# A chunked recurrence rewritten around 64x64 quadrants of TensorE, in units of eight pairs

## The chip, the cores and the metric

One core of one Trainium2 chip. The metric is the device time of one execution in microseconds; the kernel before is run three times and its median counts. Engines are named as in the profile: PE (TensorE), PEld (its weight loads), DVE (VectorE), ACT (ScalarE), POOL (GpSimd), SP (SyncE, which issues the DMAs).

## The reference

Three stages follow each other. The first is a recurrence over 768 tokens for 32 independent heads (4 batches x 8 heads), each with a 40x40 state; the other two are dense blocks over its output.

```python
for t in range(768):                       # state: [4, 8, 40, 40]
    y[t]  = r[t] @ state
    Sa    = state @ a[t]
    state = state * w[t] - outer(Sa, b[t]) + outer(v[t], k[t])
x = y rearranged to [4, 768, 320]
x = x + (gelu(x @ w_in)[u] * (w_sg @ layernorm(...)[v] + b_sg)) @ w_out   # [768 x 768] mixing over tokens
h = relu(x @ w_in2);  out = (h * sigmoid(conv3(h))) @ w_out2
```

## The kernel before

The function attention() does the recurrence, moe() the two dense blocks. The change is in attention() and in the host layout that feeds it; moe() is not touched.

The 768 tokens are cut into 12 chunks of 64. Within a chunk the recurrence becomes matrix products: decays are multiplied up along the chunk, the products of a and the decayed b and k give strictly triangular 64x64 matrices, a triangular system per head is solved, and the state is carried to the next chunk. Two heads form a pair (P = 0 and 1, on partitions 0 to 63 and 64 to 127), so there are 16 pairs; each chunk (hg) is two halves (q) of eight pairs, 24 halves in all. Two chunks form a group g (six groups), and one triangular solve serves a whole group.

- prep(hg): loads w twice (forward and reversed, tile w), a (at) and b, k (kbt); DVE runs two scans for each half (L94, L97) and multiplies at by the decay (L100); POOL multiplies kbt by the other decay (L102); ACT squares both for a range guard (L107). The tiles at are a ring of two, kbt is a ring of one.
- products(hg): PE multiplies kbt by at as 128x128 matmuls whose off-diagonal operand blocks are zero (gk, L124), DVE masks them into la (L127), PE transposes kbt (pkb, L130), ACT copies that to kbn.
- solve_a(g): DVE transposes la in 32x32 blocks (mu, L161), eliminates in 30 steps of two instructions (L168, L170), and transposes twice (tn L174, tt L176). It is a generator; each yield is a place at which the written-out order may continue with other work.
- solve_b(g, tq): PE and ACT complete the 64x64 inverse (pn L189, n L195, pt L201, tt L206), and ACT copies at into la (L207), after which the ring slot of at may be loaded anew.
- chain(g, c4): py, ys, pz, vz, pS, st (L224 to L249): the carried state of one half of a chunk; then pzt (L252). spart transposes the state (p, L262). ypart makes the output: gh (L276), ghs (L280), pyo (L285, L287), xo (L290), and stores it to x in DRAM (L295).

A list ORDER says in which order these parts are issued for one group; a scheduler then orders the instructions of each engine when the program is built, with higher priority for chain. All loads and stores go through SP's one queue.

```python
ORDER = ["chain 0", "chain 1", "g1", "sp 0", "a", "a", "a", "a", "y 0", "a", "a", "a", "sp 1", "a", "a", "y 1",
         "py0", "a", "a", "a", "chain 2", "chain 3", "a", "a", "a", "b0", "p0", "sp 2", "y 2", "g0", "sp 3", "y 3",
         "py1", "b1", "p1"]
```

Of the kernel before, what the change touches and what calls it, by code (L numbers as in the profile page):

```python
# [22 lines left out]
def attention(ctx, tc, ident, gu, wp, wr, a, kb, r, vt, v, x):  # L23
# [6 lines left out]
    D, C, J = 40, 64, 4  # L30
    NH = wp.shape[0]
# [3 lines left out]
    ps_g = ctx.enter_context(tc.tile_pool(name="ps_g", bufs=3, space=PSUM))  # L35
    ps_a = ctx.enter_context(tc.tile_pool(name="ps_a", bufs=2, space=PSUM))
    ps_c = ctx.enter_context(tc.tile_pool(name="ps_c", bufs=3, space=PSUM))
# [3 lines left out]
    p4 = ctx.enter_context(tc.tile_pool(name="a_p4", bufs=4))  # L41

    def ring(name, n, shape, val, engine, part=None):

        ts = [const.tile(shape, F32, name=f"{name}{i}") for i in range(n)]
        for t in ts:
            engine.memset(t if part is None else t[:, part:], val)
        return lambda i: ts[i % n]

    first = ring("first_", 1, [128, 8, 65], 0.0, nc.gpsimd)(0)  # L50
    rat = ring("at_", 2, [128, 16, 2, C], 0.0, nc.vector)
    rkbt = ring("kbt_", 1, [128, 16, 2, C], 0.0, nc.gpsimd)
    mask = const.tile([128, C], F32, name="mask")
    nc.gpsimd.memset(mask, 1.0)
    half = [slice(0, 64), slice(64, 128)]
    for h in half:
        nc.gpsimd.affine_select(out=mask[h], in_=mask[h], pattern=[[1, C]], compare_op=ALU.is_gt,
                                fill=0.0, base=0, channel_multiplier=-1)
    rtt = ring("tt_", 2, [128, 8, J, C], 0.0, nc.gpsimd)
    las = [const.tile([128, 2, 8, J, C], F32, name=f"la_{i}") for i in range(2)]  # L60
    rys = ring("ys_", 2, [128, 8, 2, C], 0.0, nc.gpsimd)
    rst = ring("st_", 2, [128, 8 * D + 24], 0.0, nc.gpsimd, 8 * D)
    rs0 = ring("s0_", 3, [128, 8 * D + 24], 0.0, nc.gpsimd, 8 * D)
    rr2 = ring("r2_", 3, [128, 8, 2, C], 0.0, nc.gpsimd)
    real = [slice(64 * P, 64 * P + D) for P in range(2)]
    given = [slice(64 * P, 64 * P + 48) for P in range(2)]
    rq = lambda q: slice(32 * q, 32 * q + 32)
    heads = [(i, P) for i in range(8) for P in range(2)]
    m8 = mask[:, None, None, :].to_broadcast([128, J, 2, C])

    tl, grp = {}, {}
# [4 lines left out]
    def prep(hg):  # L76

        at, kbt = rat(hg), rkbt(hg)
        px = p4.tile([128, 16, 65], F32, name="px")
        ws = []  # L80
        for src, nm in ((wp, "w1"), (wr, "w2")):
            for q in range(2):
                t = p2.tile([128, 8, 65], F32, name=nm)
                for P in range(2):
                    nc.sync.dma_start(out=flat(t)[half[P]], in_=src[hg, P, :, 520 * q:520 * q + 520])
                ws.append(t)
        for P in range(2):
            nc.sync.dma_start(out=at[given[P], :, P], in_=a[hg, P].rearrange("e (n t) -> e n t", t=C))
            nc.sync.dma_start(out=kbt[given[P]].rearrange("p n c t -> p (n c t)"), in_=kb[hg, P])
        for q in range(2):  # L90
            ns = slice(8 * q, 8 * q + 8)
            w1, w2 = ws[q], ws[2 + q]
            nc.vector.memset(first[:, :, 0], 1.0)
            nc.vector.tensor_tensor_scan(out=flat(px[:, ns]), data0=flat(w1), data1=flat(first), initial=0.0,  # L94
                                         op0=ALU.mult, op1=ALU.add)
            nc.vector.reciprocal(first[:, :, 0], px[:, ns, 64])
            nc.vector.tensor_tensor_scan(out=flat(w2), data0=flat(w2), data1=flat(first), initial=0.0,  # L97
                                         op0=ALU.mult, op1=ALU.add)
            for P in range(2):
                nc.vector.scalar_tensor_tensor(out=at[half[P], ns, P], in0=at[half[P], ns, P], scalar=-1.0,  # L100
                                               in1=px[half[P], ns, 0:C], op0=ALU.mult, op1=ALU.mult)
            nc.gpsimd.tensor_tensor(out=kbt[:, ns], in0=kbt[:, ns],  # L102
                                    in1=w2[:, :, C - 1::-1][:, :, None, :].to_broadcast([128, 8, 2, C]), op=ALU.mult)
            for i, t in enumerate((flat(px[:, ns]), flat(w2))):
                junk = p1.tile([128, 8 * 65], F16, name="junk")
                u = 4 * hg + 2 * q + i
                nc.scalar.activation(out=junk, in_=t, func=AF.Square, scale=2.0 ** -32, accum_out=gu[:, u:u + 1])  # L107
        tl[hg] = dict(px=px, at=at, kbt=kbt)

    def products(hg):  # L110

        g, tq = divmod(hg, 2)
        if tq == 0:
            grp[g] = dict(la=las[g % 2])
        la = grp[g]["la"]
        d = tl[hg]
        at, kbt = d["at"], d["kbt"]
        kbn = p4.tile([128, 16, 2, C], F32, name="kbn")
        for c in range(4):
            ns = slice(4 * c, 4 * c + 4)  # L120
            pg = ps_g.tile([128, J, 2, C], F32, name="gk", tag="pg")
            for j in range(J):
                n = 4 * c + j
# [3 lines left out]
            nc.vector.tensor_tensor(out=la[:, :, 4 * tq + c].rearrange("p P j t -> p j P t"), in0=pg, in1=m8, op=ALU.mult)  # L127
            pa = ps_a.tile([128, 4, 128], F32, name="pkb", tag="pa")
            for j in range(J):
                nc.tensor.transpose(out=pa[:, j], in_=kbt[:, 4 * c + j].rearrange("p c t -> p (c t)"), identity=ident)  # L130
            nc.scalar.activation(out=kbn[:, ns].rearrange("p n P e -> p n (P e)"), in_=pa, func=AF.Copy)  # L131
        cs = slice(4 * tq, 4 * tq + 4)
        for P in range(2):
            rows = rq(2 * P + 1)
            nc.gpsimd.tensor_copy(la[rows, P, cs, :, 0:32], la[rows, P, cs, :, 32:64])  # L135
        d.update(kbn=kbn)

    def prep_v(hg):
        vz = p2.tile([128, 2, 2, 8, D], F32, name="vz")
        for P in range(2):  # L140
            nc.sync.dma_start(out=vz[half[1 - P], P].rearrange("p q n e -> p (q n e)"), in_=v[hg, P])
        tl[hg].update(vz=vz)

    rv = {}

    def prep_y(n):
        hg, q = divmod(n, 2)
        cs = slice(512 * q, 512 * q + 512)
        r2 = rr2(n)
        zv = p3.tile([128, 8, 2, C], F32, name="zv")  # L150
        for P in range(2):
            nc.sync.dma_start(out=r2[given[P], :, P], in_=r[hg, P, :, cs].rearrange("e (n t) -> e n t", t=C))
            nc.sync.dma_start(out=zv[half[P], :, 1 - P], in_=vt[hg, P, :, cs].rearrange("e (n t) -> e n t", t=C))
        rv[n] = r2, zv

    def solve_a(g):

        la, tt = grp[g]["la"], rtt(g)
        mu = p1.tile([128, 32, 32], F32, name="mu")
        for P in range(2):  # L160
            nc.vector.transpose(out=mu[half[P]], in_=la[half[P], P, :, :, 0:32].rearrange("p c j t -> p t c j"))  # L161
        tmp = p1.tile([128, 240], F32, name="mtmp")
        for j in range(1, 31):
            if j % 3 == 0:
                yield
# [7 lines left out]
        tn = p1.tile([128, 8, J, 32], F32, name="tn")  # L173
        nc.vector.transpose(out=tn.rearrange("p c j i -> p i c j"), in_=mu.rearrange("p t i -> p i t"))  # L174
        yield
        nc.vector.transpose(out=tt[:, :, :, 32:64].rearrange("p c j t -> p t c j"), in_=mu)  # L176
        for P in range(2):
            nc.gpsimd.tensor_copy(tt[rq(2 * P), :, :, 0:32], tt[rq(2 * P), :, :, 32:64])
        grp[g].update(tt=tt, tn=tn)

    def solve_b(g, tq):

        la, tt, tn = (grp[g][n] for n in ("la", "tt", "tn"))
        cs = slice(4 * tq, 4 * tq + 4)
        pn = ps_a.tile([128, 4, J, 32], F32, name="pn", tag="pa")
        for c in range(4):
            for j in range(J):
                for P in range(2):
# [23 lines left out]
    def state(t):  # L212
        return t[:, 0:8 * D].rearrange("p (n e) -> p n e", e=D)

    def chain(g, c4):
        tq, q = divmod(c4, 2)
        hg = 2 * g + tq
        la, tt = grp[g]["la"], grp[g]["tt"]
# [92 lines left out]
    for n in range(3):  # L311
        prep_y(n)
# [491 lines left out]
```

## Time and profile before

| | |
|---|---|
| three runs | 1179.95, 1182.58, 1183.28 us; median 1182.58 |
| the profiled execution | 1181.11 us; its span 1179.4 us |
| mean granted PE clock | 0.85 of 2.4 GHz |
| busy share of the span | PE 73%, PEld 67%, DVE 63%, ACT 36%, POOL 20% |
| moved by DMA | 69.33 MB, 83,696 of 103,650 packets under 512 B |

The span is the time from the first to the last instruction of the profile; the execution's own time adds what lies around it (1.7 us here). The recurrence fills the first 682 us of the span, the dense blocks the remaining 497 us. A matmul of float32 operands appears as two records of PE and two of PEld.

### The profile page before, as it was taken

To read this page: it belongs to the slowest core of one execution; us is meant where nothing else is said; L and a number is where in the kernel's file an instruction comes from. 1 tells how busy PE (TensorE), PEld (TensorE's weight loads), DVE (VectorE), ACT (ScalarE), POOL (GpSimd) and SP (SyncE) were. 2 spreads that over 40 slices of the span, in tenths; PEclk is the share of its full clock that TensorE was granted. 3 is DMA by queue.
4 is the path that set the end of the run, shared out by engine and by line. 5 is a ranking of instruction groups with operands and counts; after the bars stand their busy time and mean duration, and the time that the engine had idled before them with its cause. 6 is when DMAs were issued, how large, how long until landed. Compare 5 with 4: busy or idle time off the path is not lost.

```text
span 1179.4 us, 23401 instructions
## 1 busy us (share of the span) xinstructions
PE 856.1 (73%) x9777; PEld 793.6 (67%) x9777; DVE 748.6 (63%) x1348; ACT 428.5 (36%) x839; POOL 236.9 (20%) x223
## 2 busy tenths in 40 slices
PE   2306670967488286929759937999999879989995
PEld 2305660856377275827758826999999879889984
DVE  6574259359746935874592267875555887776664
ACT  2302320332241133223313334432222337767764
POOL 5211101020202102020200034311111433223322
PEclk9656795879697787959788968999999989999998
DMA  9621241154233516232221195100000320000001
GB/s 160 125 54 37 48 93 34 33 105 93 61 69 61 108 28 110 62 79 59 38 64 27 29 254 150 41 1 1 1 1 1 101 78 1 34 18 18 18 17 37
DMA packets 103650, 69.33 MB, mean 59 GB/s; under 512 B 83696, under 2 KB 91376, under 8 KB 102384
## 3 DMA queue, kind: packets, MB, share of 16 engines
q1 hardware_dynamic: 103536, 67.75, 26.2%
q8 instruction: 79, 1.29, 0.5%
q14 instruction: 35, 0.29, 0.1%
HBM read 59.86 MB, written 7.86 MB: 57 GB/s over the span
## 4 chain that ended last, share of the span: by engine, by line
PE 43%; DVE 24%; DMA 13%; ACT 7%; issue 7%; POOL 3%; SPq 2%; DVEq 0%; POOLq 0%; ACTq 0%
PE pv L595 6%; PE gk L124 4%; DMA at<-in_c_a 4%; PE ph L546 3%; PE pu L577 3%; DVE mtmp L168 3%; DVE mu L170 3%; PE pr L616 3%; PE p L680 3%; PE pzt L252 3%; PE gh L276 3%; DMA w<-in_c_wp 2%; PE pz L231 2%; DVE cv L686 2%; DMA raw<-in_moe_w_in 2%
## 5 line engine op out<-in xcount | busy, mean ns | idle before, releaser
L189 PE MATMUL pn<-tn,la 32*32 32x32 f32 x768 | 18.9, 214 | 157.0 <-DVE tn L174 155.7
L189 PEld LDWEIGHTS pn<-tn,la 32*32 32x32 f32 x768 | 17.5, 129 | 159.3 <-issue 156.9
L124 PE MATMUL gk<-at,kbt 128*128 128x128 f32 x384 | 68.9, 330 | 45.7 <-POOL kbt L102 32.3
L124 PEld LDWEIGHTS gk<-at,kbt 128*128 128x128 f32 x384 | 60.4, 237 | 49.2 <-POOL kbt L102 32.7
L102 POOL TENSOR_TENSOR kbt<-kbt,w 128x1024 f32<-128x1024 f32 x24 | 56.2, 2359 | 168.6 <-DMA w<-in_c_wp 109.4
L100 DVE SCALAR_TENSOR_TENSOR at<-at,px 64x512 f32<-64x512 f32 x48 | 44.0, 952 | 66.1 <-DMA at<-in_c_a 59.0
L689 POOL TENSOR_TENSOR cv<-cv,hz 128x384 f32<-128x384 f32 x64 | 57.7, 909 | 134.6 <-ACT cv L688 134.6
L168 DVE TENSOR_TENSOR mtmp<-mu 128x30 f32<-128x30 f32 (+9 forms) x180 | 67.0, 372 | 5.0
L170 DVE TENSOR_TENSOR mu<-mu,mtmp 128x30 f32<-128x30 f32 (+9 forms) x180 | 64.8, 360 | 5.0
L207 ACT ACTIVATE la<-at 64x1024 f32<-64x1024 f32 x24 | 25.2, 1052 | 110.1 <-PE pn L189 63.1
L595 PE MATMUL pv<-sg_hi,vh 128*128 128x384 f32 x192 | 64.5, 336 | 1.0 <-ACT vh L569 1.0
L595 PE MATMUL pv<-sg_lo,vh 128*128 128x384 f32 x192 | 64.5, 336 | 0.0
L595 PE MATMUL pv<-sg_hi,vl 128*128 128x384 f32 x192 | 63.8, 336 | 0.0
L599 POOL TENSOR_TENSOR g<-g,u 128x384 f32<-128x384 f32 x32 | 36.7, 1148 | 133.2 <-DVE g L598 128.7
L135 POOL COPY la<-la 32x512 f32<-32x512 f32 x24 | 14.6, 608 | 240.7 <-DVE la L127 218.2
L693 DVE TENSOR_TENSOR gl<-cv,gh 128x384 fp32r<-128x384 f32 x64 | 40.4, 636 | 33.1 <-ACT gh L692 33.0
L280 DVE TENSOR_TENSOR ghs<-gh,mask 128x512 f32<-128x512 f32 x48 | 32.7, 682 | 44.4 <-PE gh L276 26.7
L285 PE MATMUL pyo<-r,s 128*64 128x64 f32 x704 | 56.8, 247 | 3.1 <-ACT n L195 1.9
L127 DVE TENSOR_TENSOR la<-gk,mask 128x512 f32<-128x512 f32 x48 | 33.0, 687 | 41.1 <-PE gk L124 40.9
L131 ACT ACTIVATE kbn<-pkb 128x512 f32<-128x512 f32 x48 | 28.6, 595 | 81.1 <-PE pkb L130 80.6
L287 PE MATMUL pyo<-ghs,kbn 128*64 128x64 f32 x768 | 57.0, 240 | 0.0
L684 DVE SCALAR_TENSOR_TENSOR cv<-hz,cw,cv 128x384 f32<-128x384 f32 x64 | 40.7, 644 | 25.5 <-ACT cv L683 25.4
(151 smaller groups left out, 2471.6 us busy)
## 6 DMA issues: line engine op xcount, KB each, us to landing
kbt<-in_c_kb SPq DMA_DIRECT2D x24, 384.0 KB
w<-in_c_wp SPq DMA_DIRECT2D x48, 130.0 KB
w<-in_c_wr SPq DMA_DIRECT2D x48, 130.0 KB
zv<-in_c_vt SPq DMA_DIRECT2D x48, 128.0 KB
at<-in_c_a SPq DMA_DIRECT2D x24, 192.0 KB
r<-in_c_r SPq DMA_DIRECT2D x48, 96.0 KB
raw<-in_moe_w_in SPq DMA_DIRECT2D x8, 512.0 KB
vz<-in_c_v SPq DMA_DIRECT2D x24, 160.0 KB
```

The costliest lines, as they stand in the source:

```text
L100: nc.vector.scalar_tensor_tensor(out=at[half[P], ns, P], in0=at[half[P], ns, P], scalar=-1.0, in1=px[half[P], ns, 0:C], op0=ALU.mult, op1= ...
L102: nc.gpsimd.tensor_tensor(out=kbt[:, ns], in0=kbt[:, ns], in1=w2[:, :, C - 1::-1][:, :, None, :].to_broadcast([128, 8, 2, C]), op=ALU.mult)
L124: nc.tensor.matmul(out=pg[:, j].rearrange("p P t -> p (P t)"), lhsT=kbt[:, n].rearrange("p c t -> p (c t)"), rhs=at[:, n].rearrange("p P t ...
L168: nc.vector.tensor_tensor(out=tv, in0=mu[:, j + 1:32, j:j + 1].to_broadcast([128, n, j]), in1=mu[:, j:j + 1, 0:j].to_broadcast([128, n, j] ...
L170: nc.vector.tensor_tensor(out=mu[:, j + 1:32, 0:j], in0=mu[:, j + 1:32, 0:j], in1=tv, op=ALU.add)
L285: nc.tensor.matmul(out=pyo[half[P], i], lhsT=s0s[hg, q][:, D * i:D * i + 64], rhs=r2[:, i, P], start=True, stop=False)
L287: nc.tensor.matmul(out=pyo[half[P], i], lhsT=kbn[:, 8 * q + i, P], rhs=ghs[:, j, P], start=(hg == 0), stop=True)
L595: nc.tensor.matmul(out=po, lhsT=l[:, fs], rhs=rr[:, k, cs], start=(n == 0), stop=(n == 3 * NT - 1))
L599: nc.gpsimd.tensor_tensor(out=g, in0=g, in1=us[b, c][:, f], op=ALU.mult)
L684: nc.vector.scalar_tensor_tensor(out=cv, in0=h[:, 1:N2 + 1], scalar=cw[:, 1, f:f + 1], in1=cv, op0=ALU.mult, op1=ALU.add)
L689: nc.gpsimd.tensor_tensor(out=cv, in0=cv, in1=h[:, 1:N2 + 1], op=ALU.mult)
L693: nc.vector.tensor_tensor(out=gl, in0=cv, in1=gh, op=ALU.subtract)
```

## The change

The recurrence is written anew with the same mathematics. A half of a chunk, eight pairs, is now the unit of all parts (n = 4g + c, four units in a group), and the solve still serves four units.

- Host: w (with a zero in front of each chunk), a, and interleaved b, k of a unit are laid out as one row of 2056 floats for each of 40 partitions (early), r and v likewise as rows of 1024 floats (late); the reversed copy of w is gone. A constant array pad fills the 24 unused partitions of each ring tile once.
- Decays are taken relative to the end of the chunk: a reversed scan R starts from 1, and u is the forward scan that starts from 1/R. kb is multiplied by R and a by u, both on POOL now (kb in place, a into a tile aa of seven buffers). The sign moves into the mask.
- Products without zero blocks: each 128x128 matmul becomes four of 64x64 in quadrants given by tile_position.
- chain is split: chain_v starts py from v ahead of time, chain adds the state's part. One state tile st2 is written by one DVE instruction instead of three; vz is copied by ACT alone.
- spart uses four 128x128 transposes instead of 16 matmuls. A mask covers 1024 columns in one DVE instruction where two covered 512.
- The copy of at into la is gone; the loads of a unit fill a ring of two (e) that is free again once products has read it; kbn, u, aa and f have seven buffers each.
- ORDER takes the products of all four units of the next group ahead of its solve, and chains 2 and 3 with the outputs 2 and 3 beside it; both halves of solve_b come together at its end.

```diff
+    re = [const.tile([128, EL], F32, name=f"e_{i}") for i in range(2)]
+    rl = [const.tile([128, 2, 8, C], F32, name=f"l_{i}") for i in range(3)]
...
+    def prep(g, c):
+        hg, q = unit(g, c)
+        n = 4 * g + c
+        e = re[n % 2]
+        for P in range(2):
+            nc.sync.dma_start(out=e[64 * P:64 * P + D], in_=early[hg, q, P])
...
+        nc.vector.tensor_tensor_scan(out=R[:, 519::-1], data0=w[:, ::-1], data1=flat(ones0)[:, ::-1], initial=1.0,
+                                     op0=ALU.mult, op1=ALU.add)
+        nc.vector.reciprocal(first[:, :, 0], Rn[:, :, 1])
+        nc.vector.tensor_tensor_scan(out=flat(u), data0=w, data1=flat(first), initial=0.0, op0=ALU.mult, op1=ALU.add)
+        nc.gpsimd.tensor_copy(f, Rn[:, :, 1])
+        nc.gpsimd.tensor_tensor(out=kb, in0=kb, in1=R[:, 1:521].rearrange("p (n t) -> p n t", t=65)[:, :, 1:65][:, :, None, :]
+                                .to_broadcast([128, 8, 2, C]), op=ALU.mult)
+        nc.gpsimd.tensor_tensor(out=aa, in0=a, in1=u[:, :, 0:C], op=ALU.mult)
...
+    def products(g, c):
-                nc.tensor.matmul(out=pg[:, j].rearrange("p P t -> p (P t)"),
-                                 lhsT=kbt[:, n].rearrange("p c t -> p (c t)"),
-                                 rhs=at[:, n].rearrange("p P t -> p (P t)"), start=True, stop=True)
+        G = ps2.tile([128, 2, 8, C], F32, name="gk", tag="two")
+        for n in range(8):
+            for P in range(2):
+                nc.tensor.matmul(out=G[half[1 - P], 0, n], lhsT=kb[half[P], n, 1 - P], rhs=aa[half[P], n],
+                                 start=True, stop=True, tile_position=(64 * P, 64 - 64 * P))
+            for P in range(2):
+                nc.tensor.matmul(out=G[half[P], 1, n], lhsT=kb[half[P], n, P], rhs=aa[half[P], n],
+                                 start=True, stop=True, tile_position=(64 * P, 64 * P))
+        nc.vector.tensor_tensor(out=gb[:, :, us], in0=G, in1=m2, op=ALU.mult)
...
     def solve_a(g):
-        for P in range(2):
-            nc.vector.transpose(out=mu[half[P]], in_=la[half[P], P, :, :, 0:32].rearrange("p c j t -> p t c j"))
+        nc.vector.transpose(out=mu, in_=gb[:, 0, :, 0:32].rearrange("p m t -> p t m"))
...
-            nc.scalar.activation(out=la[half[P], P, cs].rearrange("p c j t -> p (c j) t"), in_=at[half[P], :, P],
-                                 func=AF.Copy)
...
+    def chain_v(g, c):
+        for n, P in heads:
+            nc.tensor.matmul(out=py[half[1 - P], n], lhsT=rgb[g % 2][half[P], 1, 8 * c + n], rhs=d["vz"][half[P], P, n],
+                             start=(n == 0), stop=(hg == 0 and n == 7), tile_position=(64 * P, 64 - 64 * P))
...
+            nc.vector.tensor_tensor(out=st2[:, :, 0:D], in0=pS, in1=fn[:, :, None].to_broadcast([128, 8, D]), op=ALU.mult)
...
+                nc.tensor.matmul(out=pzt[half[n % 2], n // 2], lhsT=ys[half[h], D * n:D * n + 64], rhs=tt[half[h], 8 * c + n],
+                                 start=True, stop=True, tile_position=(64 * h, 64 * (n % 2)))
...
+            nc.tensor.transpose(out=p0[:, m], in_=st2[:, 2 * m:2 * m + 2].rearrange("p n e -> p (n e)"), identity=ident)
...
+    def ypart(g, c):
...
+        for n, P in heads:
+            b, m = n % 2, n // 2
+            nc.tensor.matmul(out=GH[half[P], b, m, P], lhsT=vt[half[b], m, P], rhs=r[half[b], m, P], start=True, stop=True,
+                             tile_position=(64 * b, 64 * P))
+        for n, P in heads:
+            b, m = n % 2, n // 2
+            nc.tensor.matmul(out=GH[half[1 - P], b, m, P], lhsT=zt[half[b], m, P], rhs=r[half[b], m, P], start=True, stop=True,
+                             tile_position=(64 * b, 64 - 64 * P))
...
+    ORDER = ["kv 0", "ch 0", "P 0", "G 0", "kv 1", "ch 1", "P 1", "G 1", "sp 0", "y 0", "P 2", "G 2", "sp 1", "y 1", "P 3", "G 3", "a 5", "kv 2", "ch 2", "a 4", "kv 3", "ch 3", "a 3", "sp 2", "y 2", "a 3", "sp 3", "y 3", "B 0", "B 1"]
```

## Rows read from the trace of the kernel before

**Rows 1.** The page's 40 equal slices of the span, busy share and clock in tenths

```profile
PE   2306670967488286929759937999999879989995
DVE  6574259359746935874592267875555887776664
PEclk9656795879697787959788968999999989999998
```

**Rows 2.** Stretches: length, busy us (instructions), granted PE clock, DMA share, GB/s

```profile
0.00:58.00 58.00, 17.29 (x128) 16.05 (x128) 35.15 (x45) 15.83 (x37) 24.39 (x30) 0.83 0.84 141
58.00:95.00 37.00, 0.16 (x7) 0.19 (x9) 29.25 (x71) 2.19 (x6) 4.91 (x3) 0.50 0.25 50
...
618.00:682.00 64.00, 55.28 (x1160) 50.14 (x1159) 16.91 (x27) 20.14 (x35) 2.06 (x2) 0.92 0.15 36
682.00:1179.00 497.00, 437.08 (x2401) 416.73 (x2401) 340.25 (x601) 242.01 (x480) 141.67 (x140) 0.94 0.15 44
...
310.00:345.00 35.00, 32.97 (x630) 29.24 (x632) 13.69 (x22) 12.60 (x22) 3.28 (x4) 0.89 0.18 41
345.00:374.00 29.00, 19.85 (x295) 17.31 (x287) 16.26 (x22) 10.43 (x21) 5.97 (x4) 0.71 0.52 91
374.00:415.00 41.00, 18.52 (x369) 16.95 (x369) 39.34 (x84) 8.05 (x18) 4.68 (x2) 0.77 0.43 91
```

**Rows 3.** The chain that ended last, from three windows: start, us, what

```profile
94.84 1.94 PE pn L189 x64
...
315.30 3.77 DMA at<-in_c_a
...
346.80 0.96 ACT la L207
...
348.12 7.65 DMA at<-in_c_a
...
360.69 3.78 PE gk L124 x16
...
617.89 1.94 PE pn L189 x64
```

**Rows 4.** The same chain: PE pieces at the full clock

```profile
321.89 1.12 PE gk L124 x10
330.38 0.44 PE pkb L130 x4
331.69 1.05 PE pz L231 x30
333.43 1.93 PE pzt L252 x16
338.66 1.06 PE p L262 x32
...
649.42 1.18 PE pn L189 x64
```

**Rows 5.** DVE and POOL by line: busy us, mean ns, idle before and its releasers

```profile
L168 DVE TENSOR_TENSOR mtmp<-mu 128x30 f32<-128x30 f32 (+9 forms) x180 | 67.0, 372 | 5.0
L170 DVE TENSOR_TENSOR mu<-mu,mtmp 128x30 f32<-128x30 f32 (+9 forms) x180 | 64.8, 360 | 5.0
L102 POOL TENSOR_TENSOR kbt<-kbt,w 128x1024 f32<-128x1024 f32 x24 | 56.2, 2359 | 168.6 <-DMA w<-in_c_wp 109.4 <-DMA kbt<-in_c_kb 35.3 <-DMA at<-in_c_a 11.8
L100 DVE SCALAR_TENSOR_TENSOR at<-at,px 64x512 f32<-64x512 f32 x48 | 44.0, 952 | 66.1 <-DMA at<-in_c_a 59.0 <-ACT tt L206 5.3 <-ACT s L265 1.6
L94 DVE TENSOR_TENSOR_SCAN px<-w,first 128x520 f32<-128x520 f32 x24 | 34.1, 1421 | 10.5 <-DMA w<-in_c_wp 10.1
L280 DVE TENSOR_TENSOR ghs<-gh,mask 128x512 f32<-128x512 f32 x48 | 32.7, 682 | 44.4 <-PE gh L276 26.7 <-PE pyo L287 17.6
L161 DVE STREAM_TRANSPOSE mu<-la 64x1024 f32<-64x1024 f32 x12 | 23.3, 1944 | 0.8 <-POOL la L135 0.7
L248 DVE TENSOR_TENSOR vz<-pS,px 64x320 f32<-64x320 f32 x44 | 21.5, 488 | 40.0 <-PE pS L243 39.6
```

More of the change, by code (lines that the diff above doesn't have):

```diff
@@ L46, in ring @@
         for t in ts:
-            engine.memset(t if part is None else t[:, part:], val)
+            engine.memset(t if part is None else part(t), val)
         return lambda i: ts[i % n]
[L50 to L55, printed above, removed]
+    re = [const.tile([128, EL], F32, name=f"e_{i}") for i in range(2)]
@@ L61, in attention @@
[L61 to L69, printed above, removed]
@@ L133, in products @@
         for P in range(2):
             rows = rq(2 * P + 1)
-            nc.gpsimd.tensor_copy(la[rows, P, cs, :, 0:32], la[rows, P, cs, :, 32:64])
-        d.update(kbn=kbn)
[L138 to L154, printed above, removed]
+            nc.gpsimd.tensor_copy(gb[rows, 0, us, 0:32], gb[rows, 0, us, 32:64])
@@ new lines, in attention, with prep_v, prep_y @@
+    heads = [(n, P) for n in range(8) for P in range(2)]
+    def prep_v(g, c):
+        hg, q = unit(g, c)
+        vz = p4.tile([128, 2, 8, D], F32, name="vz")
+        for P in range(2):
+            nc.sync.dma_start(out=vz[half[P], P].rearrange("p n e -> p (n e)"), in_=v[hg, q, P])
+        U[4 * g + c]["vz"] = vz
+    def prep_y(g, c):
+        hg, q = unit(g, c)
+        l = rl[(4 * g + c) % 3]
+        for P in range(2):
+            nc.sync.dma_start(out=l[64 * P:64 * P + D].rearrange("p a n t -> p (a n t)"), in_=late[hg, q, P])
+        U[4 * g + c]["l"] = l
@@ new lines, in chain @@
+                    nc.tensor.matmul(out=pS[half[P]], lhsT=ident[:, half[P]], rhs=st[:, :, 0:D], start=True, stop=False)
+            for n, P in heads:
+                nc.tensor.matmul(out=pS[half[P], n], lhsT=kbn[:, n, half[P]], rhs=vz[:, P, n],
+                                 start=(hg == 0 and n == 0), stop=(n == 7))
+            st2 = rst(2 * (hg + 1) + q)
+            fn = U[n0 + 2]["f"]
+            nc.vector.tensor_tensor(out=st2[:, :, 0:D], in0=pS, in1=fn[:, :, None].to_broadcast([128, 8, D]), op=ALU.mult)
@@ new lines, in chain @@
+            sts[hg + 1, q] = st2
+        zt = p2.tile([128, 4, 2, C], F32, name="zt")
+        for P in range(2):
+            pzt = ps1.tile([128, 4, C], F32, name="pzt", tag="one")
+            h = 1 - P
+            for n in range(8):
+                nc.tensor.matmul(out=pzt[half[n % 2], n // 2], lhsT=ys[half[h], D * n:D * n + 64], rhs=tt[half[h], 8 * c + n],
+                                 start=True, stop=True, tile_position=(64 * h, 64 * (n % 2)))
+            nc.scalar.activation(out=zt[:, :, P], in_=pzt, func=AF.Copy, scale=-1.0)
@@ L302, in run @@
             pass
[L304 to L307 removed]
+    for c in range(4):
+        prep(0, c)
+        products(0, c)
     run(solve_a(0))
[L309 to L320 removed]
+    for c in range(3):
+        prep_v(0, c)
+        prep_y(0, c)
@@ new lines, in attention @@
+            what, c = (it.split() + ["0"])[:2]
+            c = int(c)
+            last = 2 * g + c // 2 == NH - 1
+            if what == "a":
+                for _ in range(c):
+                    next(sa, None)
+            elif what == "P":
+                if more: prep(g + 1, c)
+            elif what == "G":
+                if more: products(g + 1, c)
+            elif what == "B":
+                if more:
+                    run(sa)
+                    solve_b(g + 1, c)
+            elif what == "kv":
+                with level(3): chain_v(g, c)
+            elif what == "ch":
+                with level(3): chain(g, c)
+            elif what == "sp":
+                if not last:
+                    with level(1): spart(g, c)
+            elif what == "y":
+                with level(1): ypart(g, c)
+                n = 4 * g + c + 3
+                if n < 2 * NH:
+                    prep_v(n // 4, n % 4)
+                    prep_y(n // 4, n % 4)
```

369 lines of the change are left out of this document (154 added, 215 removed).

## The prediction

> **What bounds the kernel now.** I read the page's 40 slices first, because they show where one average would mislead. The span has two parts: about 23 slices in which the digits of PE and DVE rise and fall against each other, and then slices where PE stays at 9 and the clock near its full level [rows 1]. The first part is the recurrence, up to 682 us; the second, 497 us, is the dense blocks, which the diff leaves alone. I carry those 497 us over unchanged.
>
> Next I cut the recurrence at its own landmarks. The first pn of a solve stands at 94.84 us and that of the last at 617.89 [rows 3]; four more lie between them, so five periods take 523 us, 104.6 each. The 95 us ahead are the start, the 64 us behind are the end [rows 2]. One period, from 310 to 415, falls into three stretches [rows 2]. In 310:345 PE is busy 32.97 of 35 us: PE sets the pace. In 345:374 neither is full (PE 19.85, DVE 16.26 of 29) and the clock is at a mean of 0.71. In 374:415 DVE is busy 39.34 of 41: the solve, with PE at 18.52.
>
> The chain says what the middle stretch waits for [rows 3]. The ring slot of at comes free when ACT's copy into la ends: one is followed at 315.30 by a load of 3.77 us, but the other copy runs only at 346.80, its load takes 7.65 us from 348.12, and gk follows at 360.69, at the lower clock (3.78 us for 16 records against 1.12 for 10 later [rows 4]). The products of the group's second chunk thus start 51 us after the solve before them ended, and the next solve cannot start before 374. So the period is PE work, then a late load and what hangs on it, then the solve, one behind the other.
>
> **The change part by part.**
>
> *The late load* goes: the copy of at into la is removed and the products of all four units free their input ring themselves. What is late next is the ring e of two: unit 2 is loaded after unit 0's products. One trip is load 7 us (the 7.65 above, taken a little shorter), scan 1.4, kb on POOL 2.4, aa on POOL 1.2 (half of L102's columns) [rows 5], then G and the transposes at the lower clock, about 4: 16 us. Units 0 and 1 can be loaded during the solve before, so two trips, about 35 us with mask and copies, lie beside PE's work of the same phase.
>
> *PE per unit, full clock, from [rows 4].* pz costs 1.05 us for 30 records of 64x64 quadrants, p 1.06 for 32. The split products are 64 records each for G and gh. At pz's rate they cost 2.24 us; the lower bound is pn, 64 records of small quadrants in 1.18. I take 1.7, between, because four quadrants rotate where pz rotates two. Today gk and gh are 16 records at 0.112, 1.79 each: -0.2 for both together (bounds -1.2 and +0.9). py becomes two passes: +1.2. pzt turns from 1.93 into 32 quadrant records, 1.12: -0.8. p becomes four transposes, 0.44 by pkb: -0.6. pkb, pz, pS, pyo, pn and pt keep their columns. The sum is -0.4 us a unit (-1.5 to +0.6), hence PE's 71.3 us a period (the three stretches [rows 2]) stay near 69 at the same clock.
>
> Here a rule of the Trainium skill speaks against the change. In the trace, pz's neighbouring matmuls lie in different row halves and write one PSUM bank, and cost no more per record than p, whose matmuls use all rows (1.05 for 30, 1.06 for 32 [rows 4]). "TensorEngine Tiling (Array Packing)", Restrictions and Gotchas, says that different row tiles cannot write the same PSUM bank at the same time. By the row, quadrants of both row halves go at 2.24 us per 64 records or better; by the rule they would go one behind the other, which is the third case below.
>
> *DVE per unit.* Removed: two multiplications of at (952 ns each), two of three vz/st multiplications (488 each) and a copy of vz alike. Two masks of 512 columns become one of 1024, twice (I keep 2 x 682; half of it is the lower bound). Left: two scans (1.42 at most), mask 1.37, ghs 1.37, st2 0.49, xo 0.7: 6.8 us a unit. The solve has one mu transpose instead of two of 1944 ns. Its 30 steps cost (67.0 + 64.8)/6 = 22.0 us a group; with mu and tn at 1.94 each it holds the next pn back by 26 us. Two units' st2, ghs and xo lie between its steps, 5.1 us: 31, and since 39.34 busy took 41 I put the solve phase at 34, instead of 41. PE's work beside it is two units of chain and output, about 10.2 each at the full clock: 20 to 24, hidden. [rows 2, 5] are the source.
>
> *POOL and ACT.* POOL takes aa over: 2.4 + 1.2 + about 0.8 of copies a unit, 18 us a period: hidden while it stays beside PE's phase. L100's mean of 952 ns and L102's 2359 are both DVE and POOL reading SBUF; if aa cost DVE another 1.2 us a unit on the path it would be 5 a period. I take nothing for it, and 5 as the bound. ACT loses the 0.96 us copy [rows 3] and gains small ones: nothing.
>
> *SP and DMA.* Each unit has 8 transfers instead of 15, in rows of 8 and 4 KB; DMA is busy 0.18 to 0.52 in a period [rows 2], so only latency counts, and it is in the trip.
>
> *The sum.* A period: the PE phase has 69 - 22 = 47 us of PE work at the old clock mix of 0.80; with the middle stretch's waits gone I take it at the 0.89 of 310:345, 42, and 1 for the first pn: 43. With the solve's 34 that is 77. The start: the input of unit 0 and the pads, 2.7 MB with unit 1, at 141 GB/s [rows 2] is 14 to 19 us; one trip of 16 brings unit 2, unit 3 trails by 5, products and mask take 10, the solve 26: about 70, against 95. The end: PE 55.28 of 64 us now; four units of 10.2 less what the last chunk doesn't need, with pn and pt, are 39 to 41; wall in the same proportion, 50. Together 70 + 5 x 77 + 50 = 505 instead of 682. The profiled execution took 1181.1 us (1.7 around its span); less 177 it is 1004. It stands 1.5 below the median of the three runs, so I forecast 1005.
>
> **The rivals.**
>
> *Quadrants go four at a time.* G and gh at 1.18, and a denser PE holds the full clock; the phase then ends at the two load trips, 36 us, and the solve runs at 32: 62 + 5 x 68 + 46 = 448, giving 949. For it: nothing in pz's row shows a limit at two. Against it: no row shows four at once.
>
> *Row halves do not overlap.* Then py's two passes cost 4.5 instead of 2.2 and G and gh 4.5 each instead of 1.7: +7.8 a unit. Two units of four stay hidden under the solve; the other two add 16 us at the full clock, 19 as the clock stands. The period is 77 + 19 = 96, start and end 78 and 62: 620 in all, 1120. The row of pz speaks against it.
>
> *The loads are not ahead.* SP issues in order. If the loads of a group's first units stand behind stores and late loads that wait for outputs, all four trips lie in series: 4 x 16 = 64 instead of 43, period 98, 610 in all, 1110. The late load of today is a case of this kind.
>
> *Slower.* The same place at a higher price: from 20 us a trip the phase is 80, the period 114, and 70 + 570 + 50 = 690 gives 1190. For it: a load already took 7.65 us between others, and POOL's 2.4 could wait for DVE. Against it: long rows and fewer transfers. By the Trainium skill, "DMA: Bandwidth & Descriptors", the section on why a DMA increments its semaphore by 16 ("How many engines"), a transfer uses the largest number of engines up to 16 that divides its rows, so 40 rows would go over 10 and 64 over 16. An estimate from that page: a load of e would take 1.6 times as long and a trip come near those 20 us. No row here shows the engines of one transfer.
>
> That the loads, the ring and the copies do what the diff says needs no rival; that the freed time is lost to something unseen, leaving the total within 0.3% (about 3.5 us), I give 1 in 100.
>
> **How the numbers follow.** Chances: the sum above 0.59 (its own range 960 to 1050), four at a time 0.20, row halves in series 0.08, trips in series 0.07, slower 0.05, no change 0.01. The range for 8 in 10 takes the first whole and most of the second, with POOL's 5 us a period and the lower clock at its upper side: 920 to 1085. A change of under 0.3% could not be told from none. Faster: 0.59 + 0.20 + 0.08 + 0.07 = 0.94; same 0.01; slower 0.05.
>
> **What would show it.** Periods between first pn of 77 us, of which some 34 with DVE over 9 tenths busy and 43 with PE so; no wait of DVE for a load of a inside a period; 64 records of gk in 1.2 to 2.2 us at the full clock (4.5: row halves in series); a first pn near 70; the dense blocks at 497 us. I would be wrong if POOL's waits or SP's queue show up ahead of gk, if the solve's steps are stretched by other DVE work that the scheduler puts between them, or if the granted clock stays at 0.8 in the PE phase.

## The result, and the profile after

The changed kernel ran five times: 1142.29, 1145.29, 1159.71, 1197.62 and 1206.18 us, at mean granted clocks of 0.819, 0.816, 0.799, 0.767 and 0.760; the kernel before stood at 1181.26 us (median, beside it). Ratios, here and below, are taken from the runs within 1.5% of a kernel's shortest, here two of the five: 0.9683 of the time before, interval 0.9643 to 0.9723, so at its best the kernel is some 3% faster; its two longest runs took longer than the kernel before. Even the shortest stays 137 us above my 1005 and over the range. The profile is of the longest of the five; its long stretches are checked below against profiles with higher clocks.

The 40 slices of the profile after (PE and DVE busy, granted clock and DMA share in tenths) are the counterpart of [rows 1].

```profile
span 1204.5 us, 28465 instructions
PE   1324986964795499549958935999999979989994
DVE  3594275139424912680181139775555897776664
PEclk9665665686666656555655566999999989999998
DMA  6210121122111211120110067000000320000001
```

The recurrence now ends near 705 instead of 682, and the clock digit in it, 9 in the first slice, is then mostly 5 or 6 until the dense blocks. The windows are the counterpart of [rows 2]: the start in two, then PE phases (from pn, which begins as tn ends, to the next mu) and solve phases (mu to the end of tn) in turn, the end, and the dense blocks. The expectations further down let a solve end where tn begins, 1.9 us earlier, which the next PE phase then has.

```profile
core 0: us, PE busy (x) PEld busy (x) DVE busy (x) ACT busy (x) POOL busy (x), PEclk, DMA share, GB/s
0.00:56.50 56.50, 12.21 (x308) 10.89 (x312) 23.33 (x25) 12.44 (x25) 32.70 (x41) 0.85 0.48 124
56.50:105.30 48.80, 13.16 (x272) 11.38 (x264) 43.13 (x76) 6.49 (x13) 15.88 (x17) 0.60 0.16 41
...
310.80:374.40 63.60, 60.95 (x1278) 53.30 (x1280) 14.61 (x18) 17.98 (x39) 8.87 (x11) 0.64 0.14 39
374.40:418.30 43.90, 15.22 (x434) 13.64 (x430) 38.16 (x77) 6.13 (x12) 9.20 (x11) 0.69 0.26 69
418.30:490.90 72.60, 69.42 (x1292) 60.47 (x1294) 15.79 (x20) 18.50 (x41) 11.08 (x12) 0.55 0.14 34
...
534.60:607.20 72.60, 69.45 (x1292) 60.48 (x1294) 13.36 (x18) 17.03 (x37) 7.56 (x9) 0.55 0.09 25
607.20:635.80 28.60, 11.05 (x288) 10.13 (x288) 26.44 (x69) 1.61 (x2) 0.28 (x1) 0.56 0.13 36
635.80:705.00 69.20, 62.45 (x1296) 56.79 (x1296) 11.15 (x16) 14.15 (x30) 2.06 (x2) 0.57 0.08 21
705.00:1204.00 499.00, 435.74 (x2401) 414.03 (x2401) 339.95 (x601) 241.82 (x480) 140.80 (x140) 0.94 0.15 44
```

The five PE phases take 52, 72, 64, 73 and 73 us instead of 43, with PE busy for 86 to 96% of each and the clock at 0.55 to 0.69; the five solve phases take 37, 45, 44, 44 and 29 instead of 34; the first pn stands at 105 instead of 70. The dense blocks keep their time.

DVE's groups in the solve phase 374.4:418.3 show why it isn't 34 us (columns: line, engine, operation, names, shapes, count; busy us, mean ns; idle time before them).

```profile
L159 DVE TENSOR_TENSOR mu<-mu,mtmp 128x30 f32<-128x30 f32 (+14 forms) x30 | 12.9, 431 | 0.8
L157 DVE TENSOR_TENSOR mtmp<-mu 128x30 f32<-128x30 f32 (+14 forms) x30 | 10.0, 334 | 0.8
L107 DVE TENSOR_TENSOR_SCAN u<-e,first 128x520 f32<-128x520 f32 x2 | 4.4, 2220 | 0.0
L103 DVE TENSOR_TENSOR_SCAN r<-e,ones 128x520 f32<-128x520 f32 x2 | 2.5, 1238 | 3.9 <-DMA e<-in_c_early 3.9
L289 DVE TENSOR_TENSOR ghs<-gh,mask 128x1024 f32<-128x1024 f32 x2 | 2.4, 1215 | 0.0
L135 DVE TENSOR_TENSOR gb<-gk,mask 128x1024 f32<-128x1024 f32 x2 | 2.4, 1214 | 0.0
```

Steps and output masks are as I had them. But two units of the group after it have their scans and masks here too (4.4 + 2.5 + 2.4 us), and a scan waits 3.9 us for its load, the wait that has taken the place of the load of at: DVE waits nine times for e, and SP's queue holds e back until the transposes pk have emptied the ring. The waits of DVE and of SP's queue, over the execution (what waits, for what; us in total, times, longest):

```profile
DVE r L103 <- DMA e<-in_c_early: 58.4, 9, 12.3
...
SPq L97 <- PE pk L141: 157.4, 16, 19.8
```

### The profile page after: what moved, and what is told of

It is laid out like the page before. It is cut to its first block, busy times and chain, and to the rows that moved or that the text cites. A ratio compares the mean times of both kernels' runs of the same rounds, so it can differ in the third digit from the quotient of the medians.

```text
span 1204.5 us, 28465 instructions
## 1 busy us (share of the span) xinstructions
PE 917.1 (76%) x12553; PEld 838.6 (70%) x12553; DVE 669.5 (56%) x1182; ACT 390.7 (32%) x791; POOL 274.5 (23%) x290
## 2 busy tenths in 40 slices
DMA packets 37693, 56.74 MB, mean 47 GB/s; under 512 B 19400, under 2 KB 30152, under 8 KB 35544
## 3 DMA queue, kind: packets, MB, share of 16 engines
q8 instruction: 100, 1.64, 0.6%
## 4 chain that ended last, share of the span: by engine, by line
PE 50%; DVE 28%; DMA 7%; ACT 6%; issue 4%; POOL 2%; SPq 1%; DVEq 0%; ACTq 0%; POOLq 0%
PE pv L600 6%; DVE mtmp L157 5%; DVE mu L159 5%; DMA e<-in_c_early 4%; PE pu L582 4%; PE pzt L258 3%; PE ph L551 3%; PE pz L237 3%; PE pr L621 3%; PE pS L247 3%; PE py L216 3%; PE py L229 3%; PE p L685 3%; PE pyo L301 2%; DVE u L107 2%
## 5 line engine op out<-in xcount | busy, mean ns | idle before, releaser
L128 PE MATMUL gk<-aa,e 64*64 64x64 f32 x768 | 48.9, 298 | 77.6 <-issue 32.3
L128 PEld LDWEIGHTS gk<-aa,e 64*64 64x64 f32 x768 | 42.5, 204 | 82.2 <-POOL aa L113 46.5
L301 PEld LDWEIGHTS pyo<-ghs,kbn 128*64 128x64 f32 x768 | 38.9, 185 | 52.9 <-DVE ghs L289 47.9
L103 DVE TENSOR_TENSOR_SCAN r<-e,ones 128x520 f32<-128x520 f32 x24 | 30.4, 1266 | 71.3 <-DMA e<-in_c_early 58.4
L113 POOL TENSOR_TENSOR aa<-e,u 128x512 f32<-128x512 f32 x24 | 30.4, 1265 | 162.9 <-DVE u L107 162.9
L706 PE MATMUL pq<-wv_hi,gh 128*128 128x320 f32 x192 | 42.9, 322 | 18.8 <-ACT gh L697 18.8
L110 POOL TENSOR_TENSOR e<-e,r 128x1024 f32<-128x1024 f32 x24 | 57.0, 2374 | 0.0
L138 POOL COPY gb<-gb 32x256 f32<-32x256 f32 x48 | 20.2, 420 | 157.5 <-DVE gb L135 156.0
L282 PE MATMUL gh<-l 64*64 64x64 f32 x768 | 28.7, 291 | 32.7 <-DVE gb L135 24.4
L178 PE MATMUL pn<-tn,gb 32*32 32x32 f32 x768 | 24.6, 237 | 37.8 <-DVE tn L163 37.8
```

The costliest lines, as they stand in the source:

```text
L110: nc.gpsimd.tensor_tensor(out=kb, in0=kb, in1=R[:, 1:521].rearrange("p (n t) -> p n t", t=65)[:, :, 1:65][:, :, None, :] .to_broadcast([12 ...
L128: nc.tensor.matmul(out=G[half[1 - P], 0, n], lhsT=kb[half[P], n, 1 - P], rhs=aa[half[P], n], start=True, stop=True, tile_position=(64 * P, ...
L301: nc.tensor.matmul(out=pyo[half[P], m], lhsT=kbn[:, 2 * m + b, half[P]], rhs=ghs[:, b, m, P], start=(hg == 0 and m == 0), stop=(m == 3))
L706: nc.tensor.matmul(out=acc[tt], lhsT=gs[k][g][:, 128 * tt:128 * tt + 128], rhs=rr[:, k], start=(k == 0 and n == 0), stop=(k == NF2 - 1 and ...
```

## The experiments

**One dense stream of each shape.** The kernel is nothing but float32 matmuls, 34 or 20 us of one shape at a time, with idle gaps between; it computes nothing of the reference. One shape as an example (two 64x64 quadrants, one of each row half):

```diff
+def diag_40(nc, L, X, Z, ps, k):      # two quadrants, one of each row half
+        nc.tensor.matmul(out=ps[half[r], 0:40], lhsT=L[half[r], 0:64], rhs=X[half[r], 0:40],
+                         start=True, stop=True, tile_position=(64 * r, 64 * r))
```

> Not the recurrence: eleven stretches of float32 matmuls alone on PE, each 80 to 160 groups of one shape back to back, with about 12 us of DVE copies between them while PE is idle. Theory A (shape): the granted clock rises to the full level only in the stretches of whole-array matmuls and stays at half in the stretches of 64x64 quadrants, so that 160 pairs of quadrants take about 34 us (0.107 us for each of 320 record pairs) although nothing waits. Theory B (gaps): every stretch without gaps reaches the full level after its first microseconds, whatever its shape, and 160 pairs take about 20 us; then the low clock of the changed kernel comes from waits inside its PE phase.

Measured once, by windows of this kernel (ACT does nothing in it and has no column: after PEld come DVE and POOL). In order: 128x128 products, four quadrants in rotation, one quadrant of each row half (40 columns), two quadrants of one row half, 128x64 products into alternate column halves (40 columns), 128x128 with 64 moving columns.

```profile
14.20:34.30 20.10, 19.84 (x159) 19.84 (x160) 0.66 (x4) 0.00 (x0) 1.00 0.02 6
46.60:80.90 34.30, 23.07 (x1274) 21.98 (x1278) 0.71 (x4) 0.00 (x0) 0.91 0.02 4
93.30:127.70 34.40, 34.09 (x640) 34.12 (x640) 0.62 (x4) 0.00 (x0) 0.50 0.01 3
...
186.80:221.20 34.40, 34.07 (x639) 34.10 (x640) 0.63 (x4) 0.00 (x0) 0.50 0.01 2
233.60:253.90 20.30, 19.98 (x636) 20.02 (x636) 0.62 (x4) 0.00 (x0) 0.91 0.02 4
...
299.70:334.10 34.40, 34.09 (x160) 34.12 (x160) 0.61 (x4) 0.00 (x0) 0.50 0.00 0
```

In all but the second PE is busy throughout, and yet the clock leaves its lower level (0.50 is 1.2 GHz) only in some: 128x128 products with 128 moving columns, 128x64 products in both column halves and all four quadrants rise; two quadrants don't, nor do 128x128 products with 64 moving columns. In the changed kernel py, pz, pzt and the output's state part are of the two-quadrant kind; gk and gh rotate all four.

**The changed kernel again, twice**, with no edit.

> The changed kernel once more, unedited, for a second trace and for its spread. Theory A: PE is over 9 tenths busy in its PE phase and still at half clock for most of it, and the executions differ by how much of the recurrence the full clock catches: 1140 to 1206 us. Theory B: the phases with more waits have the lower clock.

> The changed kernel itself, unedited, to see one program at several clocks. Its five first runs took 1142.29 to 1206.18 us at mean granted clocks of 0.819 to 0.760: 10.8 us for each hundredth. Theory: the clock is the cause; each run lies within 5 us of 1142 + 1085 x (0.819 - clock), and in the profile a PE phase at 0.80 or more takes 52 to 58 us and one at 0.55 some 74, with PE busy over 0.9 of the latter. Rival: the clock is low because something else holds PE up; then PE is idle for 10 us or more in the long phases and the runs leave that line.

Eight more runs: 1142.83 to 1184.58 us. Ratios: 0.9844 (0.9755 to 0.9933) and 0.9761 (0.9670 to 0.9852). The line 1142 + 1085 x (0.819 - clock), drawn through the first five runs, holds five of these eight within 5 us; the others lie 8, 8 and 14 below, so most of the spread goes with the clock, and not all. One stretch shows it without a fit: the fifth PE phase, the same part of the program as 534.6:607.2 above (the profiles differ by 46 of its PE records), in the first of these profiles.

```profile
528.20:581.80 53.60, 49.44 (x1338) 43.65 (x1338) 13.41 (x18) 17.89 (x37) 7.62 (x9) 0.84 0.12 34
```

54 us at 0.84 against 73 at 0.55, with 4 and 3 us of idle PE. So the rival (something else holds PE up) falls.

**pzt alone as quadrants, in the kernel before.**

```diff
-            nc.tensor.matmul(out=pzt[:, i], lhsT=ys[:, i].rearrange("p P e -> p (P e)"),
-                             rhs=tt[:, 2 * c4 + i // 4, i % 4], start=True, stop=True)
+            for P in range(2):
+                nc.tensor.matmul(out=pzt[half[P], i], lhsT=ys[half[P], i, P], rhs=tt[half[P], 2 * c4 + i // 4, i % 4],
+                                 start=True, stop=True, tile_position=(64 * P, 64 * P))
```

> The kernel before with one part of the change alone: pzt as two 64x64 diagonal quadrants instead of one whole-array matmul with zero blocks. PE's own work falls: 1.93 us a unit at the full clock becomes 1.1, 0.8 less, 3 us a period, up to 15 to 20 us in all if it lies on the path. Theory A: the recurrence's granted clock falls below the 0.78 of before and eats the gain: the same time or slower, by up to 30 us. Theory B: clock as before, 5 to 20 us faster.

1157.05 to 1162.87 us, 0.9843 (0.9802 to 0.9884), clock 0.851 in the profile against 0.85 before: this part alone gains about 20 us and loses no clock. Theory A missed here and theory B came true. A likely reason, not tested by itself: pzt as it was, 128x128 weights with 64 moving columns, is itself a shape that stays at the lower level in the dense streams, so nothing was taken away.

**The chain's products over 128 rows again**, step by step: pz and pzt; both passes of py too (from v and from the state); the output's state part too.

```diff
-                nc.tensor.matmul(out=pz[half[h], n], lhsT=tt[half[h], 8 * c + n], rhs=yv[half[h], n], ...,
-                             tile_position=(64 * h, 64 * h))
+                nc.tensor.matmul(out=pz[half[h], n], lhsT=tt[:, 8 * c + n], rhs=yv[:, h, n], ...)   # yv: zeros in the other half
...
```

> The changed kernel with pz and pzt alone put back on all 128 rows (zero blocks in ys, column pairs, as many matmuls and columns as before the edit; one more ACT copy a unit). The theory after the shapes run: streams of two quadrants of four (chain_v, py, pz, pzt, the first half of pyo) don't raise the granted clock, column pairs over all rows do. Two of the five parts are put back: 0 to 60 us faster than the changed kernel, granted clock above its 0.76 to 0.82. Rival (waits or the larger number of instructions hold the clock down): the clock stays where it was, and the time is the same or up to 10 us longer for the ACT copies.

> The same for the whole chain: chain_v, py, pz and pzt over all 128 rows with zero blocks (vz cleared by POOL, st and ys written in blocks: about 1 us of DVE and 0.4 us of ACT more a unit, and as many matmuls). Shape theory: the PE phase runs near the full clock, 60 us at 0.63 become about 42, period 85 to 95, total 1040 to 1100. Rival: clock as in the changed kernel, 10 to 30 us slower for the DVE and ACT work.

> rows_chain and the state part of pyo over all rows too (one more ACT copy a unit, the ring of st cut from four to two). Shape theory: at or below rows_chain, 1030 to 1090, mean granted clock 0.88 or more. Rival: as the changed kernel, 10 to 30 us slower.

> rows_all with the s0 tiles allocated anew for each unit and cleared in halves by POOL, so that an output no longer reads the state of the next chunk as it did in rows_all (the ring of two there was reused too early). The amount of work is that of rows_all, so 1145 to 1165 and a PE-phase clock of about 0.82; if the wrong order there had hidden waits, up to 20 us more.

Measured: 1161.33 to 1182.01 (0.9886, 0.9833 to 0.9939); 1161.96 to 1163.77 (0.9878, 0.9842 to 0.9913); 1150.04 to 1152.38 for the third, in which the output's state part reads the state of another chunk, at the same work on PE; 1141.39 to 1146.38 (0.972, 0.9678 to 0.9762) for the fourth, the third with the right state. Windows of the fourth, the first three PE phases and the solve after the third:

```profile
104.70:139.90 35.20, 29.70 (x838) 27.21 (x840) 12.78 (x17) 15.97 (x35) 6.33 (x10) 0.77 0.15 41
...
169.30:259.40 90.10, 70.21 (x1666) 62.21 (x1664) 30.33 (x41) 29.70 (x61) 27.99 (x38) 0.78 0.21 57
...
303.20:357.70 54.50, 51.14 (x1301) 45.72 (x1305) 18.52 (x26) 22.25 (x46) 14.80 (x25) 0.82 0.16 45
357.70:403.40 45.70, 15.33 (x444) 13.99 (x436) 40.95 (x79) 6.82 (x15) 12.64 (x15) 0.67 0.25 67
```

The shape does move the clock: these PE phases stand at 0.77 to 0.82, and the four runs of the fourth lie within 5 us where the changed kernel's own spread over 64. Pz and pzt are enough for the later phases: in the profiles of all four steps the third to fifth PE phases stand at 0.74 to 0.84, while in three profiles of the changed kernel and the one below with a third buffer they stand at 0.55 to 0.64 eight times and at 0.84 to 0.87 four times. The first step adds one ACT copy a unit, the later ones more copies and clears, so the shape changes almost alone only in the first. Over the whole execution only the third and fourth steps (0.826 to 0.833) lie above the changed kernel's best clock, 0.819. But the fourth's time is no shorter than the changed kernel's shortest run (1142.29), and the shape theory had expected 1030 to 1100 of the second and third steps. The solve phases stay as long (45.70), and the second PE phase takes 90 us (102, 100 and 87 in the three steps before). All four units of the next group are loaded in it, and three of these loads are on the chain, each some way behind the one before (start us, us, what):

```profile
178.30 6.49 DMA e<-in_c_early
...
216.78 5.91 DMA e<-in_c_early
...
233.18 5.92 DMA e<-in_c_early
```

**The ring e of three**, in the changed kernel and, with two rings made smaller for room, in the second step of the ones above.

```diff
-    re = [const.tile([128, EL], F32, name=f"e_{i}") for i in range(2)]
+    re = [const.tile([128, EL], F32, name=f"e_{i}") for i in range(3)]
...
-        e = re[n % 2]
+        e = re[n % 3]
```

> The changed kernel with three ring tiles e instead of two, nothing else. Load theory: DVE's scans wait 58 us in all for e, on the chain, because a load of 6 us starts only when the transposes of the unit two before are done; with a third tile most of that goes: 20 to 60 us faster than the changed kernel (1142 to 1206). Clock theory alone: the PE phase is set by PE at half clock, so earlier loads change nothing beyond 10 us.

> rows_chain (chain_v, py, pz, pzt over all 128 rows) with three ring tiles e (and two st and three vz tiles, to make room). If clock and loads both hold the period, each hiding behind the other: 1050 to 1110, well below either edit alone. If the clock alone counts: as rows_chain, 1155 to 1165. If loads alone count: as after_e3.

1147.71, 1154.62, 1174.25 and 1191.44 us (no interval to be had), and 1160.11 to 1167.71 (0.9892, 0.9855 to 0.9929): no gain in either. One more buffer doesn't remove the waits: with it DVE still waits 66 us for e in the changed kernel (58 without), and SP's queue 132 us for pk (157 without). That this comes of PE's order, which puts pk behind the chain, is argued here and tried in the last experiment. But the first profile, 1147.71 us, has a high clock in three of its five PE phases, with products in the shapes of the changed kernel. Its windows: first PE phase, one solve and the PE phase after it, the end.

```profile
101.30:158.30 57.00, 51.72 (x1061) 45.87 (x1063) 12.25 (x16) 16.87 (x38) 5.12 (x7) 0.59 0.11 32
...
365.70:409.60 43.90, 16.99 (x400) 15.10 (x392) 38.89 (x77) 5.36 (x12) 9.33 (x11) 0.62 0.25 69
409.60:461.70 52.10, 48.72 (x1338) 43.09 (x1338) 15.79 (x20) 19.25 (x41) 11.09 (x12) 0.87 0.17 48
...
585.20:647.00 61.80, 53.37 (x1296) 47.68 (x1296) 11.13 (x16) 13.73 (x30) 2.07 (x2) 0.69 0.10 28
```

Quadrant shapes thus don't forbid the upper level in the kernel, where other products lie between them; with them it differs from run to run.

**aa on DVE.**

```diff
-        nc.gpsimd.tensor_tensor(out=aa, in0=a, in1=u[:, :, 0:C], op=ALU.mult)
+        nc.vector.tensor_tensor(out=aa, in0=a, in1=u[:, :, 0:C], op=ALU.mult)
```

> The changed kernel with the multiplication aa on DVE (0.7 us) instead of POOL (1.27 us). Port theory: DVE's u scan (1.78 us on average instead of 1.24) and solve steps stop waiting behind POOL's aa: solve phases 2 to 4 us shorter, 10 to 25 us faster in all. Rival: DVE's 0.7 us more a unit in the solve phases eat it: within 10 us.

1187.24 to 1188.63 us, 1.0098 (1.0060 to 1.0137) of the kernel before, and inside the changed kernel's own 1142 to 1206: the gain of 10 to 25 us doesn't show, against the theory that POOL's aa, by holding up DVE, costs more than it saves. The second to fourth of the five solves in its profile take 46 us each instead of 44, where 2 to 4 less was expected. How much of the whole is the clock (0.789 in its profile) this run doesn't tell.

**What holds the period once the clock is back.** Three edits of the fourth kernel above (1142.51): both scans cut to 65 of 520 columns, which leaves the decays of the rest out; the elimination steps ahead of the next group's work; that work ahead of the chain.

```diff
+        # 1: R[:, 64::-1] for R[:, 519::-1], and u's scan over columns 0:65
...
-                    next(sa, None)
+                    with level(2): next(sa, None)                  # 2
...
-                if more: prep(g + 1, c)
+                if more:
+                    with level(4): prep(g + 1, c)                  # 3, products(g + 1, c) likewise
```

> The kernel with the products over 128 rows (1142.5 us), with both scans of every unit cut from 520 columns to 65 (the decays of the other columns are left out). Theory S: the solve phase is long because DVE, which does its elimination steps, also does the scans of the next group's units there; a unit's two scans took 1.24 + 2.22 us in the solve of 374:416, two units are in it, so the solve phases of 42 to 44 us fall to 35 to 38, and the whole by 25 to 45 us: 1098 to 1118. Rival L: the solve waits for the loads of e in series whatever the scans cost; solve phases stay over 40 and the time at 1135 to 1145.

> The same kernel, with the elimination steps of the solve given a higher priority than the next group's scans and masks, so that these go behind the solve. If the foreign DVE work in the solve is a loss by itself: solve phases 32 to 36 us, PE phases unchanged at 55, 1100 to 1115. If the work only moves, because the units' trips (load, scan, kb, products) must then be made in the PE phase: solve phases 32 to 36, PE phases 62 to 70, 1135 to 1165. If the order is set by the data and not by the priority: 1140 to 1146 with both phases as they were.

> The same kernel, with the preparation and the products of the next group given priority over the chain, so that the ring e comes free early and the four loads no longer stand behind the chain's matmuls on PE. Theory L (what is late is the load of e, issued only after the transposes pk of two units before, which PE has behind the chain): the second PE phase falls from 92 us to 60 to 70, the others from 55 to 48 to 52, 1085 to 1120. Rival: the chain is the longer string, delayed by 12 us for each unit put ahead; the PE phases stay or grow, 1140 to 1180.

Measured: 1094.71 to 1101.72 (0.9338, 0.9297 to 0.9378); 1139.32 to 1142.86 (0.9681, 0.9638 to 0.9724); 1119.78 to 1129.07 (0.9522, 0.9471 to 0.9573). A solve phase and a PE phase of the first, and of the third the second PE phase with the solve after it:

```profile
325.00:364.40 39.40, 15.34 (x398) 13.66 (x394) 35.09 (x77) 7.03 (x13) 10.14 (x13) 0.66 0.27 77
364.40:420.30 55.90, 52.87 (x1338) 46.92 (x1342) 15.79 (x28) 21.92 (x48) 16.36 (x26) 0.84 0.16 45
```

```profile
174.90:244.50 69.60, 59.00 (x1288) 52.34 (x1290) 26.78 (x32) 21.53 (x42) 20.03 (x29) 0.71 0.20 57
244.50:279.40 34.90, 26.54 (x408) 22.62 (x403) 29.96 (x70) 7.66 (x19) 6.29 (x10) 0.66 0.16 44
```

Cutting the scans is worth 42 us, as expected, though not only in the solves, where theory S had it. Against the fourth kernel's profile the first pn comes 11 us earlier, the second solve and PE phase together take 19 less (100.8 instead of 119.5), the next three solves 10 less (42.9, 39.4 and 39.9 for 43.8, 45.7 and 42.6). Priority for the steps alone changes next to nothing (2 us): in a solve of either trace the scans and masks stand between nearly the same steps, so the order hardly moved; what fixes it was not tested. Priority for the preparation takes the second PE phase from 90 to 70 us and three solves to 35 to 37, against one solve of 51 and PE phases of 61 and 66: work ahead of the chain is worth 19 us net, which misses theory L's 1085 to 1120 by a little and shows only its first sign. This version, 1123.42 us (median), beats both kernels.

## Why the prediction was wrong

The account is made on the profile at 1147.71 us, since it has the highest clocks in the PE phases and its third buffer of e gained nothing (it is in us, rounded): first pn at 101 for 70, five PE phases of 57, 69, 52, 52 and 51 (282) for 215, five solves of 41, 45, 44, 44 and 29 (202) for 170, the end 62 for 50, the dense blocks 499 for 497. These differences, 31 + 67 + 32 + 12 + 2 = 144, are what separates its span, 1146, from the 1002 of my sum.

**The step that failed** is the PE phase: "with the middle stretch's waits gone I take it at the 0.89 of 310:345, 42, and 1 for the first pn: 43". Of 69 us of PE work a period I had 22 hidden beside the solve and scaled the other 47 down to 42 by that clock. In 365.7:461.7 PE is busy 17.0 + 48.7 = 65.7 us, so the amount was nearly right. But only 17 lie beside the solve, so 48.7 are left for the phase, and they are 48.7 at 0.87, a clock at which I had 42; 3 us of waits came on top: 52. In the two phases at 0.59 and 0.70, and in all five of the profile of 1206 us, the assumed clock wasn't there at all, and a phase takes up to 73. The prediction had named this sign of being wrong ("if the granted clock stays at 0.8 in the PE phase") but put no such clock into its sum. I carried the clock of a stretch of mostly 128-row products over to quadrants as if it belonged to the stretch. It depends on what PE executes, as the dense streams show by shape and the steps back to 128 rows in the kernel, and not on that alone, since one and the same phase stood at 0.55 and at 0.84. What decides between 1142 and 1206 us for one and the same program stays open.

**Quadrants at 1.7 us per 64 records.** They go four at a time, as the first rival had it. Windows of gk alone, one unit each at the upper and the lower clock (busy of PE, PEld and DVE, then clock, DMA share and GB/s):

```profile
44.30:45.70 1.40, 0.98 (x64) 0.98 (x64) 0.00 (x0) 1.00 0.47 141
295.00:297.20 2.20, 1.99 (x64) 1.83 (x64) 0.01 (x1) 0.50 0.39 105
```

My 2.24 for the upper bound came from pz's rows of 40 columns, while gk has 64, so it was no safe bound; nothing came of it, since the price is below the lower bound. The rival's price of 1.18 was near and its result, 949, was not: "a denser PE holds the full clock" is refuted by 69 of 73 us busy at 0.55. The rival of row halves that do not overlap falls: the kernel's own quadrants of both row halves, with outputs in one bank two by two, are busy for 0.98 us per 64 where I had 4.5 for one behind the other. This doesn't agree with what the Trainium skill, "TensorEngine Tiling (Array Packing)", Restrictions and Gotchas, says: that different row tiles cannot access the same PSUM bank simultaneously.

**The solve at 34** was missing the scans and masks of two units of the group after it, and their load: I had let units 0 and 1 be loaded during the solve and put none of DVE's work for them there. In 374.4:418.3 these rows sum to 9.3 us and 3.9 of waiting, and with the 31 that stood in the working before 3 were put on top they make the 44 measured. Part is POOL's: of the two scans u in this solve one takes 1.23 us and the other, which starts within POOL's multiplication of kb, 3.21; this is of the kind that I had bounded at 5 us a period and set to nothing (start us, us, what).

```profile
394.36 1.23 DVE L107 TENSOR_TENSOR_SCAN u<-e,first 128x520 f32<-128x520 f32 x1
409.62 3.21 DVE L107 TENSOR_TENSOR_SCAN u<-e,first 128x520 f32<-128x520 f32 x1
...
409.44 2.30 POOL L110 TENSOR_TENSOR e<-e,r 128x1024 f32<-128x1024 f32 x1
```

**The loads.** One load takes 6.06 to 6.95 us in the rows below, near the 7 assumed. The estimate of 1.6 times as long by "DMA: Bandwidth & Descriptors" of the Trainium skill, "How many engines", would make 11 of the 7; no load of e in these rows comes near it. What failed is their place in the start, where "one trip of 16 brings unit 2, unit 3 trails by 5". The chain of the changed kernel's start (start us, us, what):

```profile
6.22 6.95 DMA e<-in_c_early
13.19 9.18 DMA vz<-in_c_v
26.42 6.06 DMA e<-in_c_early
...
43.54 6.38 DMA e<-in_c_early
```

Unit 3 follows unit 2 by 17 us, a whole trip, as its buffer is unit 1's and is free only after pk; and a load of vz, issued ahead of need, takes 9.18 us. Then the first solve lasts 49 us, not 26, with six scans and three masks of the next group in it. My own terms for the start also add up to 71 to 76, not 70. The rival of trips in series holds in part: in the kernel with products over 128 rows one phase with all four of them took 90 us.

**Right:** the late load of at is gone from the chain, the dense blocks are unchanged, and DMA moves 56.74 instead of 69.33 MB. The direction too, in the shorter runs; but a period at a PE-phase clock near the assumed one is 96 us (365.7:461.7) against 104.6, not 77.

## What to carry to other kernels

A clock read in a stretch belongs to the instructions of that stretch, and even then it may differ from run to run: when a change gives PE other shapes, price its phase at both levels and let the range hold both. When work is moved ahead into a phase that another engine bounds, count every instruction of it on that engine (here two scans, a mask and a load wait per unit), and follow each ring to the instruction that frees it and to what stands before that one in its queue. Where the freeing instruction stood behind the critical chain, another buffer gained nothing here; putting that work ahead gained 19 us.

## What was not expected of the hardware

Dense float32 streams of 34 us, with PE busy for 0.99 of them, stayed at 1.2 GHz (0.50) when they used two 64x64 quadrants, or 128x128 weights with 64 moving columns. Streams of 128x64 products in alternate column halves, or of all four quadrants, rose to 2.4 GHz (0.91 on average). The stream of four quadrants was then held up by something else, which stays open, at the upper clock: the timeline of PE in it (start us, us, what, idle before it).

```profile
55.02 2.09 PE L31 MATMUL ps<-X,L 64*64 64x64 f32 x128 [0.55 <-issue]
58.75 2.09 PE L31 MATMUL ps<-X,L 64*64 64x64 f32 x128 [1.64 <-issue]
```

128 records take 2.09 us, and 1.64 us pass before the next: 34 us instead of 23.
